# A weight load in three parts behind two query turns, and one difference moved from GpSimd to VectorE

## The chip, the core and the metric

The kernel runs on one core of a Trainium2 chip. The metric is the device time of one execution in microseconds. The core has a matrix engine (TensorE, PE in the profile; its weight loads are PEld), VectorE (DVE), ScalarE (ACT) and GpSimd (POOL). SyncE (SP) issues the transfers of this kernel. Each engine works through its own list of instructions in order, and waits on semaphores for what other engines or transfers must have done first. A transfer is issued by SyncE and moved by 16 DMA engines. A wait at the head of SyncE's list holds back everything behind it.

## The reference

One transformer block for 2048 tokens of width 576, with 32 heads of width 18. The conditioning vector c gives six rows that shift, scale and gate. The attention is linear, with two softmaxes as feature map, and a feed-forward part of width 4608 follows.

```python
mod = (silu(c) @ w_mod)                       # sa, ca, ga, sb, cb, gb
h   = layernorm(x) * (1 + ca) + sa
q, k, v = h @ wqkv                            # 32 heads x 18
phi(t)  = [softmax(t @ w_phi), softmax(-t @ w_phi)]
kv, z   = phi(k)^T v, sum over tokens of phi(k)
o       = (phi(q) kv) / (phi(q) z + 1e-6)
x   = x + ga * (o @ wo)
h   = layernorm(x) * (1 + cb) + sb
x   = x + gb * (relu(h @ w1) @ w2)
```

The tokens lie in 16 tiles of 128.

## The kernel before

The kernel has two stages. In the first, about 102 us long, a string of words gives the order in which the jobs of attention are written into the engines' lists. The second has eight feed-forward blocks of two token tiles each; the rest of attention for tiles 2 to 15 runs inside them.

The words that matter here:

```python
"Q": proj(q of tile t)              # TensorE: query projection into a pair of PSUM banks
"eQ": exps(...)                     # ScalarE: two exponentials, PSUM -> slot EQ[SLOT[t]]
"sq": sp.dma_start(eqd[:, u, :], EQ[:, SLOT[u], :])        # spill of tile u to DRAM
"qi": sp.dma_start(EL[:, u % NL, :], eqd[:, u, :])         # and back
"qs", "qp": sums on VectorE, ratios on GpSimd              # second softmax of tile u
"qt": sp.dma_start_transpose(ET[:, u % NET], eq(u)...)     # the turn of tile u, into RE
"kz": kv_final(0), kv_final(1)      # VectorE: masks the sums (kvz)
"nu": num_mm(t)                     # TensorE, L379: turned queries x kvz
"nO": num_o(t); "ot", "oc", "W": turn, copy, output projection
"lb", "lr", "ap", "ht", "hd", "ha": the second layernorm and its transposition
"w2a": lambda: sp.dma_start(R2[0][:], a["w2a"])            # 2.6 MB, first half of w2
"w2b": w2b_part                     # second half of w2, in three parts
"tp": lambda k: t_part(0, k)        # VectorE: a third of T1
```

SLOT has six places for the exponentials of sixteen tiles: tile 6 overwrites the slot of tile 2, and so on, so an exponential waits until the spill of the tile before it has landed. R2[0], where the first half of w2 goes, holds modulation weights until about 73.5 us. RE, where the turned queries go, holds others.

The product with w2 is computed as seven products of half-size blocks in place of eight. A11, A12 are the two hidden halves of one token tile, A22 and A2's other part belong to the second tile; B11 to B22 are the quarters of w2:

```python
def t_part(i, k):                      # L460, thirds of differences of weights, once in the kernel
    j = slice(6 * k, 6 * k + 6)
    eng, o, p, q = ((dve, T1, B12, B11), (dve, T2, B22, T1), (dve, T4, B21, T2), (dve, T3, B12, B22))[i]
    eng.tensor_tensor(out=o[:, j, :], in0=p[:, j, :], in1=q[:, j, :], op=ALU.subtract)

T_AT = {1: (3, 0), 2: (3, 1), 3: (3, 2), 6: (2, 0), 7: (2, 1), 8: (2, 2)}   # (i, k) by position in L2

def l2(b, hooks):                      # second product of block b
    ...                                # prod counts a position every 9 matmuls (L696);
    ...                                # in block 0, T_AT's parts are written there, then the hooks
    prod(X, A11, B11, al, True)                                        # positions 0, 1
    copy(0)
    dve.tensor_tensor(out=A11, in0=U2, in1=A11, op=ALU.add)            # L704
    prod(Y, A12, B21, al, True)                                        # 2, 3
    fin(t, 0, Y, 0)                                                    # L681 to L683
    pool.tensor_tensor(out=A12, in0=A12, in1=U2, op=ALU.subtract)      # L707
    prod(X, U2, T2, al)                                                # 4, 5
    copy(1)
    prod(Z, A11, T1, lo, True)                                         # 6
    prod(X, U3, T3, al)                                                # 7, 8
    copy(2)
    prod(Z, A11, T1, hi)                                               # 9
    fin(t + 1, 1, Z, 2)
    prod(X, A22, T4, al)                                               # 10, 11
    fin(t + 1, 0, X, None)
    prod(Z, A12, B22, al)                                              # 12, 13
    ...
```

The hooks of L2 do the second layernorm of the next block's tiles: statistics at positions 1 and 4, normalisation (L408) at 2 and 6, and the scaling of the turned activations (L770) at 12, all on VectorE.

Of the kernel before, what the change touches and what calls it, by code (L numbers as in the profile page):

```python
# [13 lines left out]
ALU = mybir.AluOpType  # L14
AXX = mybir.AxisListType.X

S, D, H, DH, DFF = 2048, 576, 32, 18, 4608
# [33 lines left out]
pM7 vE8 rK9 T10:1 kv6 bn12 Tc10 FQ2:2 pA9 K10:1 wl2 pM9 FQs2 FQrd2 sa12 vE9 kv7 eK10 K11:2 sp12 bn15 T12:0 kv8  # L51
sK10 Tc12 kv9 eK11 K12:1 bn14 V10:0 rK10 eK12 sK11 pA10 pM10 V11:2 vE10 rK11 QR:1 sa14 pA11 sK12 pM11 kv10 wl3
QRh V12:0 vE11 rK12 sp14 QRd pA12 kv11 pM12 vE12 T14:2 Q0:1 Tc14 wl4 K14:2 eQ0 kv12 Q1:0 eK14 qs0 Q2:1 eQ1
sK14 qp0 K15:2 eQ2 qs1 K13:0 eK15 sq2 m2:1 qp1 qi2 eK13 sK15 V13:2 w2a rK14 sK13 m2c pA14 V14:0 pM14 rK15 rK13
V15:1 vE14 pA13 pM13 vE13 Q3:0 Q4:2 eQ3 pA15 pM15 vE15 kv13 kv14 eQ4 Q5:1 qt1 sq3 kv15 eQ5 Q6:0 kz sq4 qt0 tp1
Q7:2 eQ6 sq5 tp2 nu1:3 w2b2 Q8:1 eQ7 nO1 nu0:0 tp0 eQ8 ot1:3 Q9:2 nO0 sq6 oc1 sq8 Q10:1 eQ9 sq7 ot0:0 W1:3
w2b0 oc0 eQ10 W0:2 lb1 sq9 xc1 Q11:0 lr1 lb0 w2b1 xc0 ap1 Q12:1 lr0 eQ11 ap0 ht1:3 sq10 hd1 ha1 ht0:2 sq11
Q13:0 ha0 hd0 Q14:3 eQ13 Q15:2 eQ12 sq13 eQ15 sq12 eQ14 sq15 sq14
"""

# [1 line left out]
def tile_block(ctx, tc, a, out):  # L62
# [7 lines left out]
    def small(shape, dtype, name):  # L70
        return mem.tile(shape, dtype, name=name, tag=name)

    def carve(reg, start, shape):
        n = 1
        for d in shape:
            n *= d
        names = "abcd"[:len(shape)]
        v = reg[:, start:start + n]
        return v.rearrange(f"p ({' '.join(names)}) -> p {' '.join(names)}", **dict(zip(names, shape)))
# [3 lines left out]
    R2 = [small([P, 18 * D], BF16, f"R2{i}") for i in range(2)]  # L83
# [77 lines left out]
    act, dve, pool, sp, pe = nc.scalar, nc.vector, nc.gpsimd, nc.sync, nc.tensor  # L161
# [286 lines left out]
    U2 = carve(RTh, 3 * TW, (NK, P))  # L448
    RHh = RH.bitcast(FP16)
    A11, U3, A2 = carve(RHh, 0, (NK, P)), carve(RHh, NK * P, (NK, P)), carve(RHh, 2 * NK * P, (NK, 2, P))  # L450
    A12, A22 = A2[:, :, 0, :], A2[:, :, 1, :]
# [4 lines left out]
    def t_part(i, k):  # L456
# [4 lines that stand above are left out]
# [42 lines left out]
    def h2_e(i, pr, eng):  # L503
        pt = bf(pr[:, 0, :])
        for ci in range(NC):
# [3 lines left out]
            elif ci % 2 == 0 and eng is dve:  # L509
                dve.tensor_scalar(out=o, in0=p, scalar1=mod2[:, 1, ci:ci + 1], scalar2=mod2[:, 0, ci:ci + 1],  # L510
                                  op0=ALU.mult, op1=ALU.add)

    def w2b_part(k):
        c = slice(6 * k * D, 6 * (k + 1) * D)
        sp.dma_start(R2[1][:, c], a["w2b"][:, c])
# [41 lines left out]
    def k_minus(t):  # L557
# [22 lines left out]
                                         in1=ca1[0:R, :].unsqueeze(2).to_broadcast([R, NC, FW]), op=ALU.mult),  # L580
# [15 lines left out]
        "sq": q_out, "qi": q_in, "qs": q_sm, "qp": q_pool, "qt": q_turn,  # L596
        "m2": lambda: mods([wsb, wcb], None, P, at["m2", None]), "m2c": lambda: mod2_e(at["m2", None]),
        "wo": lambda c: pool.tensor_tensor(out=wo_sb[:, c, :], in0=wo_sb[:, c, :], in1=ga_row[:], op=ALU.mult),
        "wl": w1_part, "w2a": lambda: sp.dma_start(R2[0][:], a["w2a"]), "w2b": w2b_part,
        "kz": kz,  # L600
        "nu": lambda i: num_mm(i, at["nu", i]), "nO": lambda i: num_o(i, at["nu", i]),
        "ot": lambda i: turn(o_sb[:, i, :], at["ot", i]),
# [71 lines left out]
    def fin(t, k, bank, s):  # L674

        c = slice(k * HD, (k + 1) * HD)
        y = yt[:, k, :]
        if s is None:
            dve.tensor_tensor(out=y, in0=PS[:, bank, 0:HD], in1=gb_row[:, c], op=ALU.mult)  # L679
        else:  # L680
            dve.tensor_tensor(out=y, in0=PS[:, bank, 0:HD], in1=SS[:, s, :], op=ALU.add)  # L681
            pool.tensor_tensor(out=y, in0=y, in1=gb_row[:, c], op=ALU.mult)  # L682
        pool.tensor_tensor(out=x_sb[:, t, c], in0=y, in1=x_sb[:, t, c], op=ALU.add)  # L683

    def l2(b, hooks):
        t = 2 * b
        pos = [0]

        def prod(bank, am, bm, js, first=False):
            for j in js:  # L690
                if j % 9 == 0:
                    if b == 0 and pos[0] in T_AT:
                        t_part(*T_AT[pos[0]])
                    hooks(pos[0])
                    pos[0] += 1
                pe.matmul(PS[:, bank, 0:HD], lhsT=am[:, j, :], rhs=bm[:, j, :], start=first and j == 0,  # L696
                          stop=(j % 9 == 8), skip_group_check=True)

        def copy(i):
            act.activation(out=SS[:, i, :], in_=PS[:, X, 0:HD], func=ACT.Copy)  # L700
        al, lo, hi = range(NK), range(9), range(9, NK)
        prod(X, A11, B11, al, True)
        copy(0)
        dve.tensor_tensor(out=A11, in0=U2, in1=A11, op=ALU.add)  # L704
        prod(Y, A12, B21, al, True)
        fin(t, 0, Y, 0)
        pool.tensor_tensor(out=A12, in0=A12, in1=U2, op=ALU.subtract)  # L707
        prod(X, U2, T2, al)
        copy(1)
        prod(Z, A11, T1, lo, True)  # L710
        prod(X, U3, T3, al)
        copy(2)
        prod(Z, A11, T1, hi)
        fin(t + 1, 1, Z, 2)
        prod(X, A22, T4, al)
        fin(t + 1, 0, X, None)
        sp.dma_start(outf[(t + 1) * P:(t + 2) * P, :], x_sb[:, t + 1, :])
        prod(Z, A12, B22, al)
        if b + 1 < NB:
            fin(t, 1, Z, 1)  # L720
        else:
            y, z, c = yt[:, 0, :], yt[:, 1, :], slice(HD, D)
            pool.tensor_tensor(out=z, in0=SS[:, 1, :], in1=gb_row[:, c], op=ALU.mult)  # L723
            pool.tensor_tensor(out=z, in0=z, in1=x_sb[:, t, c], op=ALU.add)
            dve.tensor_tensor(out=y, in0=PS[:, Z, 0:HD], in1=gb_row[:, c], op=ALU.mult)
            dve.tensor_tensor(out=x_sb[:, t, c], in0=y, in1=z, op=ALU.add)  # L726
        sp.dma_start(outf[t * P:(t + 1) * P, :], x_sb[:, t, :])
# [4 lines left out]
    for b in range(NB):  # L732
# [39 lines left out]

        l1(b, in_l1)
        l2(b, in_l2)

def _rows():
# [101 lines left out]
```

## Time and profile before

| What | Value |
|---|---|
| Time, median of 3 (lowest to highest) | 405.55 us (405.47 to 406.71) |
| Span of the profiled execution | 405.1 us |
| Granted TensorE clock, mean | 0.996 |
| First feed-forward matmul (L637) | 102.35 us |
| L2 of block 0, from its first matmul to the next block's first | 121.82 to 144.36 us |
| L2 of block 1, the same | 163.43 to 181.41 us |
| DMA share, 75 to 100 us | 0.92 to 1.12 |

The spans are microseconds from the first instruction. A row of the timeline is: start, length, engine, line, operation, output<-inputs, partitions x elements, type, how many of the kind in sequence; in square brackets stands how long the engine had stood idle before it, and what released it. SPq rows are issues of transfers: their length is that of the issue, not of the transfer. Matmuls are pipelined, so a busy TensorE need not be one at full pace; what counts is the spacing of its matmuls, and the granted clock beside it.

### The profile page before, as it was taken

Reading aid. Unit: us, or ns where it says so; the run is one execution under the profiler, and the core shown is the slowest. Engines: PE = TensorE matmul, PEld = TensorE weight load, DVE = VectorE, ACT = ScalarE, POOL = GpSimd, SP = SyncE. Lnnn points to the kernel's source line nnn. Section 1 sums busy time; section 2 is a strip of 40 time slices with the busy share of each in tenths; the row PEclk is TensorE's granted clock in tenths of the full one; section 3 lists DMA queues with packets and bytes.
Section 4 is the critical chain, followed back from the end, with each engine's and each line's share of the span. In section 5 each row is a group of like instructions: output and inputs, shape, how many; then the busy total and the mean of one; then the engine's idle time right before and its main releaser. Section 6 shows DMA issues by size and latency. Waiting matters only on the chain.

```text
span 405.1 us, 8867 instructions
## 1 busy us (share of the span) xinstructions
PE 391.9 (97%) x3679; PEld 315.1 (78%) x3679; DVE 246.7 (61%) x452; ACT 158.3 (39%) x359; POOL 146.0 (36%) x200
## 2 busy tenths in 40 slices
PE   8999999989999799999999999999999999999995
PEld 4677878867887588878878887888888788878884
DVE  1888997566479863755575556737655755564221
ACT  1688876678641024213410531242144114312410
POOL 2147976700111641254055106411640551072045
PEclk9999999999999899999999999999999999999999
DMA  8999134798641024133411433241154113110000
GB/s 269 368 418 417 51 118 176 285 279 342 207 105 33 18 60 104 34 32 84 76 23 48 106 45 34 60 105 33 32 87 48 20 47 60 34 32 31 2 0 32
DMA packets 48843, 44.11 MB, mean 109 GB/s; under 512 B 39249, under 2 KB 41538, under 8 KB 48162
## 3 DMA queue, kind: packets, MB, share of 16 engines
q1 hardware_dynamic: 48530, 43.36, 38.0%
q8 instruction: 29, 0.48, 0.5%
q10 hardware_dynamic: 272, 0.18, 0.1%
q14 instruction: 12, 0.10, 0.1%
HBM read 27.73 MB, written 6.49 MB: 84 GB/s over the span
## 4 chain that ended last, share of the span: by engine, by line
PE 68%; POOL 2%; DVE 1%; issue 1%; POOLq 0%; DVEq 0%
PE PS L637 30%; PE PS L696 28%; PE PS L644 4%; PE PS L398 4%; PE PS L379 1%; POOL RH L707 1%; POOL x_sb L683 1%; POOL yt L682 0%; DVE RT L460 0%; DVE yt L681 0%; POOLq L874 0%; POOL yt L723 0%; DVE xn L408 0%; DVE x_sb L726 0%; DVEq L681 0%
## 5 line engine op out<-in xcount | busy, mean ns | idle before, releaser
L637 PE MATMUL PS<-h,R 128*128 128x256 bf16 x1152 | 134.0, 273 | 0.1
L637 PEld LDWEIGHTS <-R 128*128 128x128 bf16 x1152 | 109.8, 98 | 18.2 <-issue 5.6
L696 PEld LDWEIGHTS <-RH 128*128 128x128 f16 x864 | 85.1, 99 | 25.8 <-DVE RT L460 2.2
L696 PE MATMUL PS<-R,RH 128*128 128x288 bf16 (+1 forms) x576 | 76.4, 288 | 0.0
L682 POOL TENSOR_TENSOR yt<-yt,gb_row 128x288 f32<-128x288 f32 x23 | 16.8, 730 | 165.1 <-DVE yt L681 165.1
L651 ACT ACTIVATE RH<-PS 128x256 f16<-128x256 f32 x72 | 27.6, 383 | 119.1 <-PE PS L644 112.4
L653 DVE SCALAR_TENSOR_TENSOR RH<-PS,RH 128x256 f16<-128x256 f32 x72 | 30.1, 418 | 67.9 <-ACT RH L651 67.9
L276 ACT ACTIVATE RT<-PS,rs 128x576 bf16<-128x576 f32 x64 | 42.7, 745 | 9.0 <-PE PS L271 6.2
L652 ACT ACTIVATE RH<-PS 128x512 f16<-128x512 f32 x72 | 42.9, 595 | 7.8 <-PE PS L637 6.5
L696 PE MATMUL PS<-RT,RH 128*128 128x288 f16 x288 | 39.2, 290 | 2.5 <-DVE RT L460 2.5
L700 ACT ACTIVATE RS<-PS 128x288 f32<-128x288 f32 x24 | 9.8, 410 | 76.0 <-PE PS L696 76.0
L707 POOL TENSOR_TENSOR RH<-RH,RT 128x2304 f16<-128x2304 f16 x8 | 36.4, 4547 | 0.0
L271 PE MATMUL PS<-RH,RT 116*128 116x288 bf16 x240 | 31.9, 286 | 0.4 <-DVE h L510 0.2
L271 PE MATMUL PS<-RH,R 116*128 116x288 bf16 x240 | 31.7, 286 | 0.5 <-DVE RH L467 0.3
L271 PEld LDWEIGHTS <-R 116*128 116x128 bf16 x240 | 22.9, 98 | 6.7 <-ACT R L541 0.7
L271 PEld LDWEIGHTS <-RT 116*128 116x128 bf16 x240 | 22.9, 98 | 6.5 <-DVE h L510 0.5
L408 DVE TENSOR_SCALAR xn<-x_sb,mv,rs 128x576 bf16<-128x576 bf16 (+1 forms) x28 | 22.4, 841 | 7.3 <-ACT rs L403 7.3
L238 DVE BATCH_NORM_STATS2 st<-x_sb 128x6 f32<-128x288 bf16 x60 | 24.4, 448 | 1.8 <-DMA x_sb<-in_xk_dram 1.3
L683 POOL TENSOR_TENSOR x_sb<-yt,x_sb 128x288 bf16<-128x288 f32 x31 | 22.7, 734 | 6.6 <-DVE yt L679 4.8
L281 DVE TENSOR_REDUCE Rq<-RT 128x64 f32<-128x1152 bf16 x16 | 21.5, 1344 | 3.7 <-ACT RT L276 2.2
L343 POOL TENSOR_TENSOR ratq<-Rq,rq 128x32 f32<-128x32 f32 x16 | 4.1, 253 | 53.3 <-DVE rq L340 49.5
L398 PE MATMUL PS<-wo_sb,oT 128*128 128x288 bf16 x160 | 22.4, 286 | 0.0
(112 smaller groups left out, 440.1 us busy)
## 6 DMA issues: line engine op xcount, KB each, us to landing
R<-in_w1a_dram SPq DMA_DIRECT2D x4, 1152.0 KB, 13.7
eqd<-RT SPq DMA_DIRECT2D x14, 288.0 KB, 4.5
RT<-eqd SPq DMA_DIRECT2D x14, 288.0 KB, 2.8
R<-in_w2a_dram SPq DMA_DIRECT2D x1, 2592.0 KB, 10.5
R<-in_w2b_dram SPq DMA_DIRECT2D x3, 864.0 KB, 6.9
out_dram<-x_sb SPq DMA_DIRECT2D x16, 144.0 KB, 1.8
RT<-in_xT_dram SPq DMA_DIRECT2D x2, 640.0 KB, 13.6
x_sb<-in_xk_dram SPq DMA_DIRECT2D x3, 288.0 KB, 8.4
```

The costliest lines, as they stand in the source:

```text
L238: dve.bn_stats(out=s[:, hf, :], in_=x_sb[:, t, hf * HD:(hf + 1) * HD])
L271: pe.matmul(pr[:, k, 0:HD], lhsT=xt(t, ck), rhs=w[0:R, ck, k * HD:(k + 1) * HD], start=(ck == 0), stop=(ck == NC - 1))
L276: act.activation(out=E.rearrange("p (b h s e) -> p b h s e", b=2, s=2, e=DH)[:, :, :, s, :], in_=pr[:, :, 0:HD].rearrange("p b (h e) -> p ...
L398: pe.matmul(pr[:, k, 0:HD], lhsT=oT[:, t % 2, ci, :], rhs=wo_sb[:, ci, k * HD:(k + 1) * HD], start=(ci == 0 and not add_x), stop=(ci == NC ...
L408: dve.tensor_scalar(out=o, in0=i, scalar1=mv[:, 1, t, 0:1], scalar2=rs2[:, t, 0:1], op0=ALU.subtract, op1=ALU.mult)
L637: pe.matmul(PS[:, 2 * u + hf, n * 256:n * 256 + 256], lhsT=w1a[:, ci, jj * P:(jj + 1) * P], rhs=hb[:, ci, :], start=(n == 0 and ci == 0), ...
L651: act.activation(out=A11[:, j, :], in_=lo[:, :, 0, :], func=ACT.Relu)
L652: act.activation(out=A2[:, j, :, :], in_=PS[:, 2 * u + 1, :].rearrange("p (n s f) -> p n s f", n=2, s=2), func=ACT.Relu)
L653: dve.scalar_tensor_tensor(out=U3[:, j, :], in0=lo[:, :, 1, :], scalar=0.0, in1=A11[:, j, :], op0=ALU.max, op1=ALU.subtract)
L683: pool.tensor_tensor(out=x_sb[:, t, c], in0=y, in1=x_sb[:, t, c], op=ALU.add)
L696: pe.matmul(PS[:, bank, 0:HD], lhsT=am[:, j, :], rhs=bm[:, j, :], start=first and j == 0, stop=(j % 9 == 8), skip_group_check=True)
L707: pool.tensor_tensor(out=A12, in0=A12, in1=U2, op=ALU.subtract)
```

## The change

It does two things.

In the first stage, the load of the first half of w2 is cut in three parts. The turns of query tiles 0 and 1 go in front of it in SyncE's list (they stood behind it), and the parts alternate with spills. The parts of the second half of w2 move back, and two of the three parts of T1 move to later places in VectorE's list. The purpose is that the turns and the spills don't wait behind one long load.

In block 0 of the second stage, the difference A12 - U2 is made on VectorE behind the T4 parts in place of GpSimd. The other seven blocks keep it on GpSimd. The purpose is to keep it from running beside VectorE's differences of weights.

```diff
-sK14 qp0 K15:2 eQ2 qs1 K13:0 eK15 sq2 m2:1 qp1 qi2 eK13 sK15 V13:2 w2a rK14 sK13 m2c pA14 V14:0 pM14 rK15 rK13
-V15:1 vE14 pA13 pM13 vE13 Q3:0 Q4:2 eQ3 pA15 pM15 vE15 kv13 kv14 eQ4 Q5:1 qt1 sq3 kv15 eQ5 Q6:0 kz sq4 qt0 tp1
-Q7:2 eQ6 sq5 tp2 nu1:3 w2b2 Q8:1 eQ7 nO1 nu0:0 tp0 eQ8 ot1:3 Q9:2 nO0 sq6 oc1 sq8 Q10:1 eQ9 sq7 ot0:0 W1:3
-w2b0 oc0 eQ10 W0:2 lb1 sq9 xc1 Q11:0 lr1 lb0 w2b1 xc0 ap1 Q12:1 lr0 eQ11 ap0 ht1:3 sq10 hd1 ha1 ht0:2 sq11
+sK14 qp0 K15:2 eQ2 qs1 K13:0 eK15 sq2 m2:1 qp1 qi2 eK13 sK15 V13:2 qt0 qt1 w2a0 rK14 sK13 m2c pA14 V14:0 pM14 rK15 rK13
+V15:1 vE14 pA13 pM13 vE13 Q3:0 Q4:2 eQ3 pA15 pM15 vE15 kv13 kv14 eQ4 Q5:1 sq3 kv15 eQ5 Q6:0 kz sq4
+Q7:2 eQ6 w2a1 sq5 nu1:3 Q8:1 eQ7 nO1 nu0:0 tp0 eQ8 ot1:3 Q9:2 nO0 sq6 w2a2 oc1 sq8 Q10:1 eQ9 sq7 ot0:0 W1:3
+w2b2 oc0 tp1 eQ10 W0:2 lb1 sq9 xc1 Q11:0 lr1 lb0 w2b0 xc0 ap1 tp2 Q12:1 lr0 w2b1 eQ11 ap0 ht1:3 sq10 hd1 ha1 ht0:2 sq11
 Q13:0 ha0 hd0 Q14:3 eQ13 Q15:2 eQ12 sq13 eQ15 sq12 eQ14 sq15 sq14
...
+    def w2a_part(k):
+        c = slice(6 * k * D, 6 * (k + 1) * D)
+        sp.dma_start(R2[0][:, c], a["w2a"][:, c])
...
-        "wl": w1_part, "w2a": lambda: sp.dma_start(R2[0][:], a["w2a"]), "w2b": w2b_part,
+        "wl": w1_part, "w2a": w2a_part, "w2b": w2b_part,
...
-        pool.tensor_tensor(out=A12, in0=A12, in1=U2, op=ALU.subtract)
+        if b > 0:
+            pool.tensor_tensor(out=A12, in0=A12, in1=U2, op=ALU.subtract)
...
         prod(Z, A11, T1, hi)
+        if b == 0:
+            dve.tensor_tensor(out=A12, in0=A12, in1=U2, op=ALU.subtract)
         fin(t + 1, 1, Z, 2)
```

## The prediction

> **What bounds the kernel now.** I read the busy shares and the clock row of the page first, then the chain that ended last in order of time, then the timelines of the engines where that chain leaves TensorE, and last the queue of SyncE.
>
> The page shows a kernel that is nearly all TensorE:
>
> ```profile
> PE 391.9 (97%) x3679; PEld 315.1 (78%) x3679; DVE 246.7 (61%) x452; ACT 158.3 (39%) x359; POOL 146.0 (36%) x200
> ...
> PEclk9999999999999899999999999999999999999999
> ```
>
> Only 405.1 - 391.9 = 13.2 us of the span are without a matmul, and one slice of forty, the fourteenth (131.6 to 141.8 us), has a lower granted clock. A change off TensorE can only win where TensorE waits or runs slow. The chain, asked for 128 to 150 us, shows where that is:
>
> ```profile
> 128.77 6.63 PE PS L696 x54
> 135.40 0.03 issue
> 135.43 0.02 DVEq L681
> 135.45 1.72 issue
> 137.16 0.63 DVE xn L408 x2
> 137.79 0.97 DVE RT L460
> 138.76 0.04 issue
> 138.81 5.55 PE PS L696 x30
> 144.36 3.06 PE PS L637 x28
> ```
>
> Columns: start, length, what. TensorE runs 54 matmuls in 6.63 us (0.123 us each), stops at 135.40, and then needs 5.55 us for 30 more (0.185 each). The timeline of the other engines says why it stops:
>
> ```profile
> 131.78 4.55 POOL L707 TENSOR_TENSOR RH<-RH,RT 128x2304 f16<-128x2304 f16 x1
> 131.88 5.36 DVE L460 TENSOR_TENSOR RT<-R,RT 128x1728 f16<-128x1728 bf16 x1
> ```
>
> The GpSimd difference A12 - U2 of the first block starts 0.1 us ahead of a VectorE difference of weights (T4), whose five sisters take 1.05 us. This one takes 5.36: it ends at 137.24, which is the end of GpSimd's (136.33) plus 0.91. TensorE's product with T4 (the one that starts at 135.40) stands behind it. Stretches of 1 us give the clock afterwards (columns: stretch, length, busy of the five engines with counts, clock, DMA share, GB/s):
>
> ```profile
> 139.00:140.00 1.00, 1.00 (x8) 0.58 (x7) 1.00 (x2) 0.00 (x0) 0.00 (x0) 0.71 0.82 163
> 140.00:141.00 1.00, 1.00 (x6) 0.64 (x5) 0.09 (x1) 0.00 (x0) 0.75 (x2) 0.50 0.00 0
> 141.00:142.00 1.00, 1.00 (x6) 0.64 (x5) 0.52 (x2) 0.00 (x0) 0.71 (x1) 0.50 0.00 0
> 142.00:143.00 1.00, 1.00 (x7) 0.62 (x6) 1.00 (x3) 0.00 (x0) 0.76 (x1) 0.58 0.00 0
> ```
>
> So the stop costs twice: the idle time, and a half clock for some 3.5 us. The second place where TensorE waits is the first use of the turned queries:
>
> ```profile
> 85.54 0.55 PE L379 MATMUL PS<-kvz,RE 128*128 128x76 bf16 x10 [1.14 <-DMA RE<-RT]
> ...
> 88.01 0.55 PE L379 MATMUL PS<-kvz,RE 128*128 128x76 bf16 x10 [0.69 <-DMA RE<-RT]
> ```
>
> and SyncE's queue shows why the turns are late (start, length of the issue):
>
> ```profile
> 73.85 0.38 SPq L599 DMA_DIRECT2D R<-in_w2a_dram  x1
> 74.33 6.57 SPq L347 DMA_TRANSPOSE RE<-RT  x1
> 81.00 1.00 SPq L333 DMA_DIRECT2D eqd<-RT  x2
> 82.05 3.32 SPq L347 DMA_TRANSPOSE RE<-RT  x1
> ```
>
> The 2.6 MB load is issued at 73.85. The turn of tile 1 comes right behind it, and its issue alone takes 6.57 us where a turn in a later block takes 1.30; it holds back two spills and the turn of tile 0. The load lands 10.5 us after its issue (84.4), the first turn 11.2 us after its own (85.5, where TensorE resumes).
>
> **What the Trainium skill says.** SBUF — State Buffer, Who interferes with whom: a VectorE instruction with two SBUF inputs contends with a GpSimd instruction that reads SBUF; it is an exclusive lock, and whoever issues first makes the other block for the whole instruction. The trace agrees: 5.36 us against 1.05, with GpSimd 0.1 us ahead. TensorE: Matmul & The Clock Gate, What's actually happening: after an idle window (about 3.4 us, free-running) the array's clock falls to 4/8 and comes back after about one busy window. The trace shows 0.50, for some 3.5 us, after two gaps (1.91 and 0.60 us) that are together shorter than that window, so the size is taken from the trace. DMA: Bandwidth & Descriptors, Queues, rings and completion order: on each DMA engine the descriptors of a queue are consumed in ring order. The 11.2 us of the turn behind the 2.6 MB load, against a median of 4.0 for the four turns between 70 and 125 us, agree.
>
> **The change part by part: the sum on VectorE.** Removed: 4.55 us of GpSimd in block 0. Added: one VectorE difference 128x2304 in f16. VectorE has such a shape already (L704, 1.30 us in this block), so 1.3 us. It stands after the third T4 part. VectorE then runs, from the end of the statistics at 131.9: T4 part 0 (1.05, to 132.9), normalise (0.63, to 133.6), T4 parts 1 and 2 (2.0, to 135.6), the difference (1.3, to 136.9), then the close of Z (0.45, to 137.3). TensorE reaches T4 part 0 at 135.40 (ready at 132.9) and part 2 twelve matmuls later, 135.40 + 12 x 0.123 = 136.9 (ready at 135.6). It reaches A12 and Z after 18 matmuls, at 137.6 (ready at 136.9 and 137.3). All are in time, by 0.3 us or more. The next block's activations are normalised at 133.6 in place of 137.8 and turned by 137 or so; their scaling takes 1.8 us on VectorE and is queued behind the close of X (137.6 + 0.5), so it ends near 139.9, when TensorE needs it at 139.8: within some tenths, as in the later blocks.
>
> The gain, worked out twice. From the chain: TensorE stands from 135.40 to 144.36, which is 8.96 us for 36 matmuls that need 36 x 0.123 = 4.4, so 4.5 us. From the blocks: L2 of block 0 takes 144.36 - 121.82 = 22.54 us, L2 of block 1 (the same matmuls, from 163.43 to 181.41) 17.98, so 4.56. I take off 0.1 for the scaling: **-4.4 us**. Some 2.8 of it is idle time and 1.7 is clock.
>
> **The loads and turns.** Both turns move in front of the load. Their inputs are ready when GpSimd has ended the second query tile (72.28 + 1.17 = 73.45) and the modulation matmuls have read the buffer (about 73.5). At 1.3 us of issue each they are out by 76.5 and land by about 80. TensorE comes to them at about 84.4 and VectorE's masking of the sums (kvz) ends at 82.84, so both waits go: up to 1.14 + 0.69 = 1.83 us. The first spills after them land earlier too, so the exponentials that reuse their slots are not held.
>
> The load itself loses nothing on this path: part 0 is issued at 76.6; 885 KB at the 430 GB/s of the stretch 75 to 80 us are 2.1 us, so it lands near 81 and is used near 86. Parts 1 and 2 go out near 81.6 and 85, land near 87 and 90, and are used near 88 and 94. The second weight (w2b) is complete near 98 by the same rate (3.5 MB and three spills from 85.5 on); its reader stands at 113, so there are 15 us to spare.
>
> What is given back: VectorE's second and third difference of T1 (1.05 us each) move to later places. The second falls into a hole (2.60 us idle at 89.8, waiting for a copy). The third now stands between the two normalisations that used to run back to back (95.65, 2.17 us), and the transposition of tile 0 already waited 0.38 us for the second of them. It is 1.05 us later against a TensorE that is 1.8 us earlier, so I expect its wait to grow from 0.4 to about 1.3. Net 1.83 - 0.9 = about **-1.0 us**. The count of matmuls is unchanged.
>
> Sum: 405.55 - 4.4 - 1.0 = 400.15, rounded to **400.1 us**.
>
> **The rivals.**
>
> 1. The idle time goes, but ScalarE's exponentials become the bound of the end of attention: ScalarE is busy 18.6 of the 23 us between 82 and 105, and the first feed-forward block needs the banks that the last four pairs free. For: no engine but TensorE is fuller there. Against: ScalarE has holes of 1.61 and 0.98 us there which end with matmuls and a spill. Then the turns bring 0 to 0.5 us: 400.7 to 401.2.
> 2. A part of the load arrives late and holds VectorE, which is in order, so the statistics behind it wait. For: the DMA engines are at a share of 0.92 to 1.12 from 75 to 100 us, and a third more of the load is now in that stretch. Against: some 1 us of room on part 1 and 4 on part 2. A stall of 1 to 2 us: 401 to 402; if TensorE stops for 2 us the half clock is added, 403.
> 3. The sum on VectorE only shifts the wait: Z's close is now behind it, and the product that needs A12 follows. Room 0.3 us at Z. If VectorE is some tenths late, TensorE stops for tenths, without the half clock: block 0 brings 4.0 in place of 4.4.
> 4. Everything in attention moves up by the whole 1.83 us, as tile 0's transposition is hidden by other matmuls: 399.2.
>
> **Range and chances.** Block 0 gives 4.0 to 4.6, the turns -0.5 to 1.9, and the runs of before alone spread over 1.2 us. Eight times in ten: 398.8 to 402.2. Two per cent are 8.1 us (below 397.4), more than all TensorE waits that the change touches, 4.56 + 1.83 = 6.4: 0.04. Slower by 2%: 0.01.
>
> **What would show it.** In the changed kernel: no GpSimd operation over 4 us in the first block; every T4 difference at 1.05 us; a clock of 1.00 through 139 to 143 us; L2 of block 0 near 18.0 us. For the turns: no wait of the L379 matmuls for a DMA before 90 us; the first feed-forward matmul near 101.3 in place of 102.35; a wait of about 1.3 us before the transposition of tile 0. I am wrong if VectorE waits for a weight DMA between 85 and 97 us, if TensorE waits for ScalarE at the start of the feed-forward, or if the half clock appears at another place.

## The result, and the profile after

| | before | changed |
|---|---|---|
| Time, median (lowest to highest) | 405.51 us (405.40 to 406.71), 4 runs | 403.36 us (402.45 to 403.74), 4 runs |
| Ratio, 95% interval | | 0.9937 (0.9911 to 0.9963) |
| Again, beside experiments | 406.07 us, 35 runs | 403.65 us, 9 runs: 0.9937 (0.9916 to 0.9958) |

The change makes the kernel 2.2 to 2.4 us faster, not 5.4. The measured time lies above the predicted range.

The stop in block 0 is gone, wholly. The page, and the chain from 125 us on:

```profile
PE 389.2 (97%) x3677; PEld 314.4 (79%) x3679; DVE 243.9 (61%) x453; ACT 158.1 (39%) x359; POOL 141.6 (35%) x199
...
PEclk9999999999999999999999999999999999999999
```

```profile
127.57 1.23 PE PS L398 x10
128.79 11.03 PE PS L700 x90
139.82 3.06 PE PS L641 x28
```

(Lines of the changed kernel have other numbers: L700 was L696, L641 was L637, L657 was L653.) The 54 and 30 matmuls that had a gap of 3.4 us between them are one row of 90 now, 0.123 us each. VectorE's timeline shows the T4 part and the moved difference:

```profile
131.90 1.00 DVE L460 TENSOR_TENSOR RT<-R,RT 128x1728 f16<-128x1728 bf16 x1
132.82 0.63 DVE L408 TENSOR_SCALAR xn<-x_sb,mv,rs 128x576 bf16<-128x576 bf16 x2
133.37 2.02 DVE L460 TENSOR_TENSOR RT<-R,RT 128x1728 f16<-128x1728 bf16 x2
135.31 1.35 DVE L720 TENSOR_TENSOR RH<-RH,RT 128x2304 f16<-128x2304 f16 x1
```

A T4 part takes 1.00 us in place of 5.36, and the difference 1.35 where GpSimd needed 4.55.

The waits for the turned queries are gone too, but TensorE has a new one. Its timeline, with the idle time in brackets:

```profile
84.35 0.54 PE L379 MATMUL PS<-kvz,RE 128*128 128x76 bf16 x10
...
96.59 0.48 PE L501 MATMUL PS<-ident,xn 128*128 128x128 bf16 x5 [0.89 <-DVE xn L408]
...
101.31 3.22 PE L641 MATMUL PS<-h,R 128*128 128x256 bf16 x28
...
111.34 0.60 PE L641 MATMUL PS<-h,R 128*128 128x256 bf16 x4 [1.13 <-DVE RH L657]
```

The feed-forward starts at 101.31 us, 1.04 earlier than before. Nine microseconds later it stops for 1.13 us, and L2 starts at 121.77, where it started before (121.75 in the same view). VectorE, which TensorE waits for, waits itself for the read-back of query tile 3. Its sum over that tile opens what I call the closing of a tile: the second softmax behind the read-back, and then the turn.

```profile
109.26 1.35 DVE L281 TENSOR_REDUCE Rq<-RT 128x64 f32<-128x1152 bf16 x1 [2.55 <-DMA RT<-eqd]
```

In the profile before, this sum began at the same time behind a shorter wait:

```profile
109.24 1.35 DVE L281 TENSOR_REDUCE Rq<-RT 128x64 f32<-128x1152 bf16 x1 [1.48 <-DMA RT<-eqd]
```

TensorE came later then and did not notice. SyncE's list in the changed kernel shows why the read-back did not move:

```profile
91.29 0.98 SPq L519 DMA_DIRECT2D R<-in_w2b_dram  x2
92.69 12.68 SPq L333 DMA_DIRECT2D eqd<-RT  x6
105.47 1.95 SPq L336 DMA_DIRECT2D RT<-eqd  x2
```

It stands behind the last spill, which waits for ScalarE's last exponential. ScalarE waits for the spill that frees a slot, and that spill stands behind three weight parts (issued at 88.45 and from 91.29 on):

```profile
102.38 2.64 ACT L276 ACTIVATE RT<-PS,rs 128x576 bf16<-128x576 f32 x4 [0.70 <-DMA eqd<-RT]
```

So the chain to test is: weight part, spill, exponential, last spill, read-back, VectorE, TensorE.

### The profile page after: what moved, and what is told of

The parts are those of the page before. It is cut to its first block, busy times and chain, and to the rows that moved or that the text cites. A ratio compares the mean times of both kernels' runs of the same rounds, so it can differ in the third digit from the quotient of the medians.

```text
span 400.3 us, 8872 instructions
## 1 busy us (share of the span) xinstructions
PE 389.2 (97%) x3677; PEld 314.4 (79%) x3679; DVE 243.9 (61%) x453; ACT 158.1 (39%) x359; POOL 141.6 (35%) x199
## 4 chain that ended last, share of the span: by engine, by line
PE 68%; POOL 2%; DVE 0%; issue 0%; POOLq 0%; DVEq 0%
PE PS L641 30%; PE PS L700 28%; PE PS L648 4%; PE PS L398 4%; PE PS L379 1%; POOL RH L712 1%; POOL x_sb L687 1%; POOL yt L686 0%; DVE yt L685 0%; POOLq L881 0%; POOL yt L730 0%; DVE x_sb L733 0%; DVEq L685 0%; POOLq L730 0%; POOLq L712 0%
## 5 line engine op out<-in xcount | busy, mean ns | idle before, releaser
L641 PE MATMUL PS<-h,R 128*128 128x256 bf16 x1152 | 133.7, 273 | 1.1 <-DVE RH L657 1.1
L641 PEld LDWEIGHTS <-R 128*128 128x128 bf16 x1152 | 109.8, 98 | 18.8 <-issue 6.4
L700 PEld LDWEIGHTS <-RH 128*128 128x128 f16 x864 | 84.5, 98 | 21.8
L700 PE MATMUL PS<-R,RH 128*128 128x288 bf16 (+1 forms) x576 | 75.6, 286 | 0.0
L657 DVE SCALAR_TENSOR_TENSOR RH<-PS,RH 128x256 f16<-128x256 f32 x72 | 30.1, 418 | 67.8 <-ACT RH L655 67.8
L700 PE MATMUL PS<-RT,RH 128*128 128x288 f16 x288 | 37.9, 286 | 0.0
L712 POOL TENSOR_TENSOR RH<-RH,RT 128x2304 f16<-128x2304 f16 x7 | 31.8, 4547 | 0.0
```

The source lines that it names most:

```text
L641: pe.matmul(PS[:, 2 * u + hf, n * 256:n * 256 + 256], lhsT=w1a[:, ci, jj * P:(jj + 1) * P], rhs=hb[:, ci, :], start=(n == 0 and ci == 0), ...
L657: dve.scalar_tensor_tensor(out=U3[:, j, :], in0=lo[:, :, 1, :], scalar=0.0, in1=A11[:, j, :], op0=ALU.max, op1=ALU.subtract)
```

## The experiments

Fifteen kernels were run. "Order" is the new order of loads, turns and T1 parts; "sum" is the difference on VectorE. Ratios are to the kernel before, run beside them on the same chip. In the traces I measure stretches from the first modulation matmul (near 72 us): the stages ahead of it start up to 1.9 us apart from one execution to the next. One execution of each kernel was profiled, and it need not be a typical one.

| Kernel | Time, us | Ratio (95%) |
|---|---|---|
| sum alone | 402.43 | 0.9907 (0.9888 to 0.9926) |
| order alone | 406.86 | 1.0023 (1.0009 to 1.0037) |
| changed, late closing of tile 3 | 401.81 | 0.9889 (0.9867 to 0.9911) |
| that, and T1's third part in a hole | 401.89 | 0.9896 (0.9875 to 0.9917) |
| changed, again | 403.65 | 0.9937 (0.9916 to 0.9958) |
| sum alone, late closing | 402.44 | 0.9906 (0.9877 to 0.9935) |
| changed, load whole behind the turns | 405.99 | 0.9992 (0.9975 to 1.0010) |
| changed, spills first | 402.62 | 0.9926 (0.9900 to 0.9952) |
| changed, early read-back | 402.33 | 0.9892 (0.9868 to 0.9916) |
| early read-back, late closing, hole | 402.19 | 0.9907 (0.9878 to 0.9936) |
| changed, sum on VectorE in all blocks | 403.68 | 0.9934 (0.9910 to 0.9958) |
| all mended, w2b late | 402.06 | 0.9923 (0.9900 to 0.9946) |
| changed, w2b late | 406.53 | 1.0015 (0.9997 to 1.0034) |
| all mended, spill of tile 5 first | 401.54 | 0.9900 (0.9876 to 0.9925) |
| sum alone, again | 402.78 | 0.9926 (0.9905 to 0.9946) |

### The two parts one by one

**The sum alone**: the kernel before, with

```diff
-        pool.tensor_tensor(out=A12, in0=A12, in1=U2, op=ALU.subtract)
+        if b > 0:
+            pool.tensor_tensor(out=A12, in0=A12, in1=U2, op=ALU.subtract)
...
         prod(Z, A11, T1, hi)
+        if b == 0:
+            dve.tensor_tensor(out=A12, in0=A12, in1=U2, op=ALU.subtract)
```

> Only the difference A12 - U2 of block 0 goes to VectorE; loads, turns and T1 parts stay as before. Theory A (the stop of block 0 is all of the gain, idle time surely and half clock in some executions): L2 of block 0 takes 18.0 us in place of 22.5, and the time is 401.0 to 402.7 us, at or below the changed kernel's 403.4. Theory B (the two parts of the change need each other, or the order brings a share of its own): 404 us or more. Theory C (the profile of before showed a half clock that most executions don't have, so only the idle part counts): 402.5 to 403.5.

402.43 us against 405.79: 3.4 us, more than the whole change brings. Theory B falls. L2 of block 0, from its first matmul to the first one of the next block, takes 17.88 us in the trace, as A said:

```profile
121.53 1.26 PE L696 MATMUL PS<-R,RH 128*128 128x288 bf16 x9
...
139.41 3.22 PE L637 MATMUL PS<-h,R 128*128 128x256 bf16 x28
```

What tells A from C is the mean granted clock of each execution. Over the four sets that were run beside experiments, the kernel before shows 0.996 or less in 39 of 95 executions, with a median of 406.92 us, and 0.999 or more in 55, with 405.63. Of the 18 executions in the old order with the sum on VectorE, so without the stop, none shows 0.996 or less. So the half clock goes with the stop, but only two executions in five have it. In this set the two groups are 406.84 and 405.55 us; the sum alone is below them by 4.4 and by 3.1.

**The order alone**: the changed kernel, with the difference back on GpSimd in block 0.

> Only the order of loads, turns and T1 parts is changed; the difference stays on GpSimd. Theory A (what attention gains is given back in the first feed-forward product, where VectorE waits for the read-back of query tile 3): first feed-forward matmul at 101.3 us, first matmul of L2 at 121.8 as before, time 405.0 to 405.8, the same as before. Theory B (the order is worth its 1.0 us): 404.5, and L2 starts at 120.7.

406.86 us: neither. The order costs 1.1 us by itself. It does so in executions with a mean clock of 0.999 or more (406.50 against 405.55 us) and in those with 0.996 or less (408.06 against 406.84). The profiled execution (404.75 us, the fastest of 22) has the stop, and behind it the full clock (columns as before, the clock is third from the end):

```profile
135.00:136.00 1.00, 0.00 (x0) 0.00 (x0) 1.00 (x1) 0.00 (x0) 0.67 (x1) 1.00 0.00 0
136.00:137.00 1.00, 0.36 (x3) 0.31 (x4) 1.00 (x3) 0.00 (x0) 0.00 (x0) 1.00 0.00 0
137.00:138.00 1.00, 0.55 (x5) 0.29 (x3) 1.00 (x2) 0.00 (x0) 0.00 (x0) 1.00 0.00 0
138.00:139.00 1.00, 0.85 (x6) 0.58 (x6) 1.00 (x3) 0.00 (x0) 0.00 (x0) 1.00 0.67 135
```

```profile
121.09 1.26 PE L700 MATMUL PS<-R,RH 128*128 128x288 bf16 x9
...
142.05 3.23 PE L641 MATMUL PS<-h,R 128*128 128x256 bf16 x28
```

L2 of block 0 takes 20.96 us here, 22.45 in the profile before (same view) and 17.88 without the stop. So the stop costs 3.1 us at the full clock and 1.5 us more where the half clock follows; the executions gave 3.1 and 4.4. The idle gaps, 1.91 and 0.60 us, are the same in both traces. This trace does not show where the order loses its 1.1 us: L2 starts 49.32 us after the first modulation matmul, in the profile before 49.61. The trace of a longer execution, at the end of the experiments, does.

**The changed kernel again**

> The changed kernel once more, beside the others on one chip. Theory A (the 402.5 us of its first profile was its best case, and the wait of VectorE for the read-back of query tile 3, 2.5 us there, varies with the transfers): 402.9 to 403.8 us, the profile's stop of TensorE in the first feed-forward product 1.1 to 2.3 us. Theory B (the difference to the kernel with the sum alone, 402.4, is one of chips): 402.4 or less.

403.65 us: Theory A. In its profile (402.64 us, the fastest of 9) TensorE stops for 1.62 us in the first feed-forward product:

```profile
109.48 1.35 DVE L281 TENSOR_REDUCE Rq<-RT 128x64 f32<-128x1152 bf16 x1 [3.04 <-DMA RT<-eqd]
```

The feed-forward began at 100.45 us there, still earlier than in the first profile, and VectorE's sum of tile 3 began no earlier than there. What TensorE gains it waits for.

### The wait for the read-back

**Late closing**: VectorE closes tile 3 one step later in block 0.

```diff
-            if (g, u) in ((0, -1), (0, 1)):
-                q = t0 + max(u, 0)
+            if (g, u) in ((0, -1), (0, 2 if b == 0 else 1)):
+                q = t0 + (u > 0)
```

> The changed kernel, and in block 0 the closing of query tile 3 on VectorE stands one step later (behind the third relu group in place of the second). Theory A (the wait for the read-back holds VectorE and through it TensorE): the wait of 1.13 us of the first feed-forward matmuls is gone, L2 starts at 120.7, time 1.0 to 1.3 us below the changed kernel's, near 402.2. Theory B (the turned query itself is late): the wait moves to the L379 matmuls near 119, and the time stays within 0.3 us of the changed kernel.

401.81 us, ratio 0.9889 against 0.9937, with intervals that do not overlap: Theory A by the time. TensorE's wait for VectorE is gone. VectorE still waits 1.61 us for the read-back, but the work that TensorE needs stands ahead of it. A new wait of 0.47 us for ScalarE shows in front of the last banks. The profile, of the longest execution (402.29 us), does not show L2 at 120.7, as A wrote, but at 121.72. Still, counted from the first modulation matmul, its read-back is 1.1 us later than in the changed kernel's second profile (VectorE's sum at 38.68 against 37.57), and L2 starts 0.35 us sooner (49.73 against 50.08).

**The same on the sum alone**

> The order of before, the sum on VectorE, and the closing of query tile 3 one step later. Theory A (the old order has a wait of 0.36 us there, the new one 1.13 and more): 0.2 to 0.5 us below the sum alone, 401.9 to 402.2. Theory B (the late closing helps only where the new order has made the wait long): 402.4, the same as the sum alone.

402.44 us: Theory B. In the old order TensorE's wait there was only 0.36 us. The new order makes that wait long.

**Early read-back**: a fourth place for read-back tiles (the zeros of the start-up lie in h2 in its stead), and the read-back of tile 3 ahead of the last spills.

```diff
-    NEQ, NE, NV, NL = 6, 5, 4, 3
+    NEQ, NE, NV, NL = 6, 5, 4, 4
-... nO0 sq6 w2a2 oc1 sq8 Q10:1 eQ9 sq7 ...
+... nO0 sq6 w2a2 oc1 sq8 qi3 Q10:1 eQ9 sq7 ...
-    zero = small([P, 512], BF16, "zero")
+    zero = h2[:, 1, 0:2, :].rearrange("p a b -> p (a b)")
-    for u in range(QF + 1, QF + NL):
+    for u in range(QF + 2, QF + NL):
```

> The changed kernel with a fourth place for read-back tiles, so that the read-back of query tile 3 stands behind the spill of tile 8 in SyncE's list and not behind the last spill. Theory A (the read-back is late because it stands behind the last spills, which ScalarE's last exponentials set): no wait of VectorE for a read-back from 100 to 112 us, the first feed-forward product without a wait for VectorE, time 1.4 to 2.0 us below the changed kernel's 403.65, at a ratio of 0.989 to before. Theory B (with that wait gone, the next one, ScalarE's last exponentials or the late closing of tile 2, takes its place): 403.2 to 403.7, ratio 0.993.

402.33 us, ratio 0.9892: the size that Theory A gave. VectorE's sum of tile 3 follows its neighbour without a wait:

```profile
108.17 0.42 DVE L657 SCALAR_TENSOR_TENSOR RH<-PS,RH 128x256 f16<-128x256 f32 x1 [0.41 <-ACT RH L655]
108.51 1.34 DVE L281 TENSOR_REDUCE Rq<-RT 128x64 f32<-128x1152 bf16 x1
```

A wait of 0.79 us for another read-back appears at 111 us, in a place where it doesn't stop TensorE. TensorE has a wait of 0.81 us for ScalarE in the first feed-forward product instead, a part of what Theory B named. So two independent ways, calling later or delivering earlier, take the same loss away.

### What makes spills and read-back late

**The load whole behind the turns**

```diff
-... V13:2 qt0 qt1 w2a0 rK14 ...
+... V13:2 qt0 qt1 w2a0 w2a1 w2a2 rK14 ...
```

(with w2a1 and w2a2 taken out of their later places)

> The changed kernel, but the three parts of the load are issued one behind the other directly after the two turns, so that the transfers of 76 to 82 us are full again. Theory A (the change leaves the DMA engines with too little to move from 74 to 80 us, 129 GB/s in place of 285, and the moved bytes delay the spills and the read-back after 95): the wait on a weight part on VectorE is gone, the wait of the first feed-forward product for VectorE is 0.5 us or less, time 0.5 to 1.0 below the changed kernel. Theory B (long loads ahead of the spills hurt more than a late end): ScalarE waits 2 us or more for spills from 84 to 90, and the time is the same or higher.

405.99 us: Theory B. One long load ahead of the spills holds ScalarE, which holds TensorE (the profiled execution is the longest, 409.02 us):

```profile
90.28 2.64 ACT L276 ACTIVATE RT<-PS,rs 128x576 bf16<-128x576 f32 x4 [5.95 <-DMA eqd<-RT]
```

```profile
91.71 4.96 PE L271 MATMUL PS<-RH,RT 116*128 116x288 bf16 x20 [5.30 <-ACT RT L276]
```

TensorE stops for 5.30 us, and its next 20 matmuls take 4.96 us where such a group takes 2.62; 17 of 22 executions have a mean clock of 0.9965 or less. This is what the three parts are for: turns in front need a load that lets spills through.

**Spills first**: late closing; w2a1 behind sq3, w2a2 behind sq5, sq7 ahead of sq8, the second and third T1 parts later, one part of w2b behind the turn of tile 2, the spill of tile 10 ahead of the exponentials of tile 11, and the T2 parts in the third group.

> The late closing, spills in front of weight parts where both are ready, the second and third part of T1 in VectorE's later holes, one part of w2b behind the turn of query tile 2 with the T2 parts in the third group. Theory A (the waits of 85 to 110 us are those of spills behind weight parts): the waits of TensorE for ScalarE near 91 and 105 us shrink from 0.8 and 0.7 to 0.3 or less each, time 0.5 to 1.5 below the kernel with the late closing, 400.3 to 401.3. Theory B (the DMA engines are full there, and another order only moves the waits): within 0.4 us of 401.8.

402.62 us: above both ranges, so no gain, which is nearer to Theory B. In the profile (404.10 us) TensorE's wait moved to 89 us (1.90, for ScalarE, which waits 2.5 for a spill), and the T2 parts in the third group cost 1.15 at the start of L2. The first feed-forward product itself had no wait.

**w2b late**: the changed kernel, with only two parts of w2b moved.

```diff
-... lr1 lb0 w2b0 xc0 ap1 tp2 Q12:1 lr0 w2b1 eQ11 ... ht0:2 sq11
-Q13:0 ha0 hd0 Q14:3 eQ13 Q15:2 eQ12 sq13 eQ15 sq12 eQ14 sq15 sq14
+... lr1 lb0 xc0 ap1 tp2 Q12:1 lr0 eQ11 ... ht0:2 sq11 w2b0
+Q13:0 ha0 hd0 Q14:3 eQ13 Q15:2 eQ12 sq13 eQ15 sq12 w2b1 eQ14 sq15 sq14
```

> The changed kernel with only this difference: two parts of w2b stand behind the spills of tiles 11 and 12. Theory A (the weight parts ahead of the spills cost the order its gain): ScalarE's wait near 102 us is gone, the last spill and the read-back are 0.7 to 3 us earlier, the wait of VectorE for the read-back is about 1.5 us, time 402.0 to 402.8, ratio 0.990. Theory B (only the place of the read-back in SyncE's list matters): the same as the changed kernel, 403.4 to 403.9, ratio 0.993 to 0.994.

406.53 us: both wrong. ScalarE's wait is gone, as A said; weight parts ahead of spills do hold it. But one part of w2b now stands directly ahead of the last two spills and the read-back, and the wait grew there:

```profile
110.86 1.35 DVE L281 TENSOR_REDUCE Rq<-RT 128x64 f32<-128x1152 bf16 x1 [4.35 <-DMA RT<-eqd]
```

TensorE stopped for 2.93 us, even in this shortest execution (404.02 us); 12 of 14 executions have a clock of 0.9965 or less. So the read-back decides here, and the weight part ahead of it delays it.

**All mended, w2b late**: early read-back, late closing, T1's third part in the hole, and the same two parts of w2b.

> The early read-back, the late closing of tile 3, the third T1 part in the later hole, and two parts of w2b moved behind the spills of tiles 11 and 12. Theory A (ScalarE's last four exponentials wait for spills that stand behind three weight parts): ScalarE's wait of 2.6 us before them and TensorE's of 1.65 us for ScalarE are gone, first feed-forward product 19.1 us long, time 400.3 to 401.2, ratio 0.986. Theory B (the spills land late because the DMA engines are full whatever the order): the waits stay above 1 us and the time above 401.8.

402.06 us. In the profile (401.18 us, the shortest) the waits are gone as A said (no wait of TensorE from 99.2 to 118 us), but the time is above A's range. Small ones take their place: 0.43 us at 118, 0.67 at 122 for the transposition of an output tile.

**The spill of tile 5 first** (on the kernel before this one: sq5 w2a1 in place of w2a1 sq5, T1's second part in the hole, its third at the end of attention)

> As the first of this set, and the spill of tile 5 in front of the second part of the load, the second T1 part in the hole of the third and that at the end of attention. Theory A (the wait of ScalarE of 1.2 to 1.8 us near 89 is for that spill behind that part): the wait is gone, and with it TensorE's of 0.3 to 0.8 near 91; 0.3 to 0.8 us below the first of this set. Theory B (the wait near 89 is hidden by later ones): the same within 0.3 us.

401.54 us, 0.5 below the last, the size that A gave; the wait near 89 is gone, but one of 1.27 us for ScalarE stands at 96. The intervals (0.9876 to 0.9925, 0.9900 to 0.9946) overlap too far to call it settled.

**The sum alone, on the same chip**

> The sum alone once more, on the chip of the others. If it and the kernels with the order mended lie apart by 0.6 us or more, the order has a worth of its own; if not, the sum is all that the change brings. Expected: 402.4, ratio 0.9907.

402.78 us. The mended orders lie 0.7 and 1.2 us below it (late closing and sum alone on one chip earlier: 0.6). By the medians the order is worth 0.6 to 1.2 us once its waits are mended, by the ratios 0.1 to 1.1; the intervals of the ratios overlap, so the sign is likely and the size is not shown.

### Two other questions

**T1's third part in the hole** (tp2 behind hd1 in place of ap1, on the late closing; the hole is a stretch in which VectorE idles, 1.64 us in the first profile)

> As the kernel with the late closing, and the third part of T1 stands between the scalings of tile 1 and tile 0 in place of between the two normalisations. Theory A (that part delays the transposition of tile 0): the wait of 0.89 us before it falls to about 0.1, the feed-forward starts 0.6 to 0.9 us earlier, time 0.5 to 0.9 below the kernel with the late closing. Theory B (ScalarE's exponentials bound the end of attention): a wait for ScalarE appears at the first feed-forward matmuls, and the time is the same within 0.3.

401.89 against 401.81: Theory B. The wait of 0.89 us before the transposition of tile 0 is gone, and the feed-forward starts 0.9 us earlier, but TensorE then waits 0.69 us for ScalarE's last exponentials.

**With the early read-back as well**

> The early read-back, the late closing of tile 3 and the third T1 part in VectorE's later hole together. Theory A (each takes away a wait of TensorE of its own): below the early read-back alone by 0.3 to 0.8 us, near 401.2. Theory B (ScalarE bounds the end of attention, so the earlier transposition only makes TensorE wait for ScalarE): the same as the early read-back within 0.3 us.

402.19 against 402.33: Theory B again. TensorE waits 1.65 us for ScalarE at the start of the feed-forward, 0.81 with the early read-back alone:

```profile
103.82 2.64 ACT L276 ACTIVATE RT<-PS,rs 128x576 bf16<-128x576 f32 x4 [2.65 <-DMA eqd<-RT]
```

ScalarE isn't full there; it waits for a spill.

**The sum on VectorE in all blocks** (`if b > 0` with GpSimd taken out, the VectorE line for every b)

> The changed kernel with the difference on VectorE in all eight blocks. Theory A (GpSimd's difference costs only where a VectorE operation that TensorE needs soon starts behind it, which is block 0): the normalisation beside it falls from 2.9 us to 0.6 in blocks 1 to 6, TensorE's pace is unchanged, time within 0.4 us of the changed kernel. Theory B (it delays the next block's activations in other blocks too, as the 0.4 us longer first matmuls of block 2 hint): 0.5 to 2 us lower.

403.68 us, as the changed kernel: Theory A. The normalisation beside it falls from 2.89 to 0.64 us in block 1, and block 1 keeps its 37.04 us. In this kernel GpSimd's lock costs something only where TensorE needs what is behind it.

This run answers one more thing. Up to L2 of block 0 it runs as the changed kernel does, and its profile is that of a long execution (405.06 us, where the first profile of the changed kernel has 402.45). So it shows where a long execution of the new order loses its time:

```profile
104.41 2.64 ACT L276 ACTIVATE RT<-PS,rs 128x576 bf16<-128x576 f32 x4 [2.98 <-DMA eqd<-RT]
```

```profile
105.83 0.60 PE L641 MATMUL PS<-h,R 128*128 128x256 bf16 x4 [1.99 <-ACT RT L276]
...
113.81 0.60 PE L641 MATMUL PS<-h,R 128*128 128x256 bf16 x4 [1.71 <-DVE RH L657]
```

The last part of w2b lands 10.5 us after its issue, where it took 9.1 in the first profile. ScalarE waits 2.98 us for a spill (0.70 there), TensorE 1.99 us for ScalarE, VectorE 3.12 us for the read-back, and TensorE 1.71 us for VectorE. Counted from the first modulation matmul, L2 starts 2.1 us later than in the first profile, which is most of the 2.6 us between the two executions.

## Why the prediction was wrong

**The sum: mechanism right, size right for one kind of execution.** Lock, T4 at 1.05 (1.00), difference at 1.3 (1.35), clock of 1.00, L2 of 18.0 (17.89): all came as written. The term "-4.4 us" was 3.0 to 3.4 by the medians of the sum alone. It holds 1.7 us of half clock (1.5 measured), which I took from one profile of an execution that ran 406.93 us, and subtracted from a median of 405.55 us of executions of which most don't have it. The three times given before, 405.47, 405.55 and 406.71, already showed two groups. That step is 1.0 to 1.4 us of the miss.

**The loads and turns: wrong in sign.** Turn waits gone, feed-forward at 101.31 (101.3 predicted), tile 0 waiting 0.89 us (1.3 predicted): right. The step that failed is "Net 1.83 - 0.9 = about **-1.0 us**", which takes a feed-forward that starts 1.0 us earlier for a kernel that ends 1.0 us earlier. The runs show about +1.0 in its place (order alone 1.0023, which is 0.9 to 1.1 us; the changed kernel 0.9937 against 0.9907 and 0.9926 for the sum alone, 0.4 to 1.2 us), so this is about 2 us of the miss. In the traces the changed kernel's feed-forward starts 0.8 us earlier than that of the sum alone, counted from the first modulation matmul, and L2 of both starts at 49.52 us. What I left out is the next appointment on the path: VectorE's closing of tile 3, which in the profile before already waited 1.48 us for its read-back and so had no slack to give. Late closing and early read-back each win the loss back, which shows it.

That explains the loss of the gain. For the change to be slower than the sum alone, something must be later than before as well. A second step of the prediction failed there: "so the exponentials that reuse their slots are not held". In the first profile the early ones were held for 1.25 us at 89.42 (0.98 at 93.29 before), and the late ones, which the prediction didn't look at, cost more. In the six traces with the changed kernel's order of loads and spills, ScalarE waits 0.38, 0.70, 1.44, 1.47, 1.69 and 2.98 us for a spill before its last four exponentials; in the four traces of the old order it does not wait there. The last spill, the read-back and the last banks of the first feed-forward product stand behind these exponentials. The weights landed later than the prediction had them: the parts of the first half at 83.3, 88.6 and 92.2 us (it said near 81, 87 and 90), the second half at 100.8 (near 98).

The moved bytes fit (start:end, then as above, last DMA share and GB/s), first before, then changed:

```profile
74.00:80.00 6.00, 6.00 (x60) 4.88 (x58) 3.40 (x4) 2.80 (x10) 5.41 (x12) 1.00 0.98 370
...
100.00:105.00 5.00, 4.80 (x43) 3.84 (x41) 2.46 (x5) 5.00 (x9) 1.42 (x2) 1.00 0.36 138
```

```profile
74.00:80.00 6.00, 6.00 (x58) 4.87 (x56) 3.52 (x5) 2.78 (x11) 5.29 (x12) 1.00 1.09 165
...
100.00:105.00 5.00, 4.92 (x48) 4.12 (x50) 1.63 (x3) 4.30 (x8) 1.42 (x2) 1.00 0.67 255
```

Before, 370 GB/s x 6 us = 2.2 MB moved from 74 to 80 us; in the changed kernel 165 x 6 = 1.0 MB: with the two turns under way the DMA engines are as busy (1.09) with fewer bytes. The 1.2 MB come back from 80 us on, 0.6 of them from 100 to 105, among the spills that the read-back waits for. I looked at the readers of the weights ("15 us to spare") and not at the spills that would queue behind the weights. That weight parts ahead of the spills make ScalarE wait, and a part ahead of the last spills delays the read-back, is shown by the kernel with w2b late. That a long execution of the new order loses its time on this chain is shown by the trace of 405.06 us. That the 1.2 MB are why the spills land late is argued, not shown: to move them early again, with the load whole behind the turns, made the kernel slower.

**The rivals.** The first (ScalarE as a bound) and second (a late part) had the waits at the right places but not the cause: VectorE waited only 0.55 us for a weight part, at 88.65 us, and ScalarE waits for spills. The wait for a weight part is on the prediction's list of signs of being wrong. So is TensorE's wait for ScalarE at the start of the feed-forward, which came too: none of note in the first profile, 0.43 us in the second, 1.99 in the long execution. The third didn't occur. The fourth was wrong.

**Still open.** In the kernel before, the time is 1.8 us above the span; in the changed kernel 2.2, in the sum alone 1.9, in the order alone 2.0. So 0.2 to 0.4 us of the order's loss lie outside the first-to-last instruction, and no run says why. Nor does a run say why the last part of w2b lands later in one execution than in another.

## What to carry to other kernels

A wait that is removed is worth the room up to the next appointment: follow the earlier start to the next wait on each engine that feeds the path, and read how long that wait is already in the profile before; here VectorE's 1.48 us for a read-back was the warning that an earlier TensorE would find VectorE waiting. When a load is moved, look at what stands behind it in the transfer queue and not only at who reads it. And take a profile's size from the executions that the median stands for: where a stop may or may not bring a half clock, the removed stop is worth its idle time always and the clock only as often as it occurs.

## What the runs showed of the hardware that was not expected

A TensorE stop of 1.91 and 0.60 us brought the half clock in two of five executions (39 of 95, by their mean clock) and cost 1.5 us more in the trace where it did. The Trainium skill (TensorE: Matmul & The Clock Gate, What's actually happening) gives a free-running window of about 3.4 us; a stop shorter than the window that trips it in some executions only is not what the page leads one to expect, and the measurement decides.

The issue of a turn has no fixed length. The two turns ahead of the weights took 4.03 us to issue in the first profile of the changed kernel and 2.81 in the run with the sum in all blocks; single turns later in the first profile took 1.28 to 1.96. The prediction's 1.3 us each was the low end. From 74 to 80 us the moved bytes were 165 GB/s at a DMA share of 1.09, so a full share is no measure of bytes while transposing transfers run.
